# Turning the mix result over by four DMA transfers per unit instead of three GpSimd copies, one turn before its split

## The chip, the cores and the metric

The kernel runs on one NeuronCore of a Trainium2 chip. The metric is the device time of one execution in microseconds (us); the value of a kernel is the median of its runs. Five engines work side by side, each through its own list of instructions in order: TensorE (PE, with its weight loads as PEld), VectorE (DVE), ScalarE (ACT), GpSimd (POOL) and SyncE (SP). SP computes nothing here: it issues DMA transfers, one after the other, and an issue that has to wait for something holds up every issue behind it.

## The reference

A Fourier layer (real FFT over the sequence, a complex 256 x 256 mix with a soft threshold, inverse FFT) is followed by a token-shift channel mix and a second feed-forward with a mish activation:

```python
X = np.fft.rfft(x, axis=1)                       # x: 4 x 3072 x 256
Yr = Xr @ w_r - Xi @ w_i + b_r
Yi = Xr @ w_i + Xi @ w_r + b_i
Yr = np.sign(Yr) * np.maximum(np.abs(Yr) - lam, 0.0)   # Yi likewise
y = np.fft.irfft(Y, n=3072, axis=1)
...
k = np.maximum(xk @ w_k, 0.0); v = k * k @ w_v; r = sigmoid(xr @ w_r); x = r * v
...
h = x @ w_in; out = (h * np.tanh(softplus(h))) @ w_out
```

## The kernel before

The time falls into three stages: the first 302 us compute the Fourier layer up to the first half of the inverse transform, the rest computes the channel mix and then the last feed-forward. The change touches the first stage alone. A forward FFT of 3072 = 96 x 32 points is done in two steps of matrix products (`s1` over 96 rows, `s2` over 32), the inverse likewise (`is1`, then `is2`). Between `s1` and `s2`, and between `is1` and `is2`, the data goes through DRAM (`scr1`, `scr2`), which turns its layout. Every product of the first stage except `s1` is done in a split form: ACT rounds a tile to a high part (`Xh`, `Ah`, `Yh`), DVE computes the rest (`Xl`, `Al`, `Yl`), and PE multiplies high by high, high by low and low by high.

The work between the two DRAM passes is cut into 48 units (`NU`), 12 for each of 4 batches, and the loop at L687 runs one turn per unit, with several units in flight. In turn u, in the order of the program:

- `s2(u + 1)` (PE); `is1_ev(u - 3)` copies the inverse product of an earlier unit out of PSUM to `Cs` (ACT) and stores it to `scr2` (SP, L449); `s1_ev` evicts and stores a tile of a later batch;
- `s2_ev(u + 1)` splits the result of `s2` into `Xh` (ACT) and `Xl` (DVE); two steps of background work (`bg`, below);
- `load_A(u + 5)` (SP, L333) and `split_A(u + 3)`;
- `mix(u)`: the products with the mix weights and the bias (PE), `K1` (ACT) and the sum `yt` (DVE, L406);
- `split_Y(u - 1)`: `Yh` (ACT, L77) and `Yl` (DVE, L78); `above(u)`: `yc` (ACT, L411); `shrink(u)`: the soft threshold `Y` (DVE, L417) and its rearrangement;
- in 20 of the turns `s1` of a tile of a later batch with `load_x` (SP, L276); `is1(u - 2)` (PE, L436); two more steps of `bg`; from turn 33 on one step of `early`, which already loads and prepares the first tiles of the second stage.

The rearrangement is what the change is about. After `shrink`, `Y` holds in 128 partitions x 2 x 256 four quarters of 64 partitions x 256, and `is1` needs the upper quarter of column block 0 and the lower quarter of column block 1 exchanged. Three GpSimd copies through a helper tile `sw` do it in place (L419 to L421).

Two tables set the order around this. `bg` takes the weights of the second stage from a queue, one at a time: a DMA of 512 KB into `dec_raw` (SP, L111) in one step, then four steps later, one turn of the loop, the first of seven DVE instructions that decode it (L118 to L137), then the split (L97, L99). There are nine such weights in this stage, so nine DMAs, each issued in the last step of a turn (turns 4, 8, ... 36) and first read on DVE in the last step of the next turn, right behind `shrink`. `early(0)` in turn 33 loads `Dp`, `D` and `ift` (L457, L471, L252), `early(1)` splits two of them in turn 34.

PSUM holds one buffer for `s2` and one for `is1`, so PE starts `s2` of the next unit only when `Xl` of the last one has been read out, and `is1` only when `Cs` has been copied.

Of the kernel before, what the change touches and what calls it, by code (L numbers as in the profile page):

```python
# [8 lines left out]
F32 = mybir.dt.float32  # L9
# [4 lines left out]
ALU = mybir.AluOpType  # L14
# [3 lines left out]
B, S, D, FK, FF = 4, 3072, 256, 1024, 2048  # L18
N1, N2 = 96, 32
NG = 12  # L20
NU = B * NG
# [4 lines left out]
LAM = 0.01  # L26
# [3 lines left out]
def kernel(  # L30
# [27 lines left out]
    nc = tc.nc  # L58
# [13 lines left out]
    def split(src, hi, lo, lo_eng=None, hi_eng=None):  # L72

        if hi_eng is nc.vector:
            nc.vector.tensor_copy(out=hi, in_=src)
        else:
            nc.scalar.copy(out=hi, in_=src)  # L77
        (lo_eng or nc.vector).tensor_tensor(out=lo, in0=src, in1=hi, op=ALU.subtract)  # L78
# [6 lines left out]
    def bg(n):  # L85

        while n > 0 and bgq:
            try:
                next(bgq[0])
                n -= 1  # L90
            except StopIteration:
                bgq.popleft()
# [63 lines left out]
    p1p = p1.__enter__()  # L156
# [20 lines left out]

    def load_consts():
        def t(tag):
            return p1p.tile([128, 512], F32, tag=tag, name=tag, bufs=1)  # L180

        if not cst:
            cst["m"] = t("dec_raw")
            nc.sync.dma_start(out=cst["m"], in_=c_mw)
            return
        cst["x"] = [t("yt"), t("yc")]
        for v, w in zip(cst["x"], (w_r, w_i)):
            nc.sync.dma_start(out=v.rearrange("p (h n) -> p h n", h=2), in_=w.rearrange("(h p) n -> p h n", p=128))
# [17 lines left out]

    def split_mix():
        r, i = cst["x"]
        d = [p1p.tile([128, 512], F32, tag="T", name="wd", bufs=2) for _ in range(2)]
        nc.vector.scalar_tensor_tensor(out=d[1], in0=r, scalar=-1.0, in1=i, op0=ALU.mult, op1=ALU.subtract)  # L210
        nc.vector.tensor_tensor(out=d[0], in0=i, in1=r, op=ALU.subtract)
        for c, v in ((0, r), (2, d[1]), (1, d[0])):
            v = v.rearrange("p (h n) -> p h n", h=2)
            split(v, WX[:, :, c, 0, :], WX[:, :, c, 1, :])
# [64 lines left out]
    def load_x(b, q):  # L279
        new_x(b, q)  # L280
        for _ in x_loads(b, q):
            pass

    def warm(n):
        z = p1p.tile([128, 512], F32, tag="yt", name="zero", bufs=1)
        nc.vector.memset(z[:, 0:256], 0.0)
        p = ps1p.tile([128, 2, 512], F32, tag="s2", name="warm", bufs=1)
        for _ in range(n):
            nc.tensor.matmul(out=p[:, 0, 0:256], lhsT=z[:, 0:128], rhs=z[:, 0:256], start=True, stop=True)
# [34 lines left out]
    def gview(scr, g):  # L324

        return scr.rearrange("s n d -> (s n) d")[256 * g:256 * (g + 1)].rearrange("(e p) d -> p e d", e=2)
# [3 lines left out]
    def load_A(u):  # L330
        b, g = divmod(u, NG)
        t = p1p.tile([128, 2, D], F32, tag="A", name="A", bufs=4)
        nc.sync.dma_start(out=t, in_=gview(scr1a if u < 4 else scr1[b], g))  # L333
        A_t[u] = t
# [7 lines left out]
    def s2(u):  # L342
        last = u % NG == GS
        hl = Ah.pop(u)
        p = ps1p.tile([128, 2, 512], F32, tag="s2", name="s2p", bufs=1)
        for dh in range(2):
            v = p[:, dh, 0:384].rearrange("p (c e j) -> p c e j", c=3, e=2)
            for e in range(2):
                mc = MC[:, int(last and e == 1)]
                for i, (a, w) in enumerate(((0, 0), (0, 1), (1, 0))):  # L350
                    nc.tensor.matmul(  # L351
                        out=v[:, :, e, :], lhsT=hl[a][:, e, dh * 128:(dh + 1) * 128],
                        rhs=mc[:, w, :], start=(i == 0), stop=(i == 2),
                    )
        s2_t[u] = p
# [22 lines left out]
    mx_t, Y_t = {}, {}  # L378

    def mix(u):  # L380
        hl = Xh.pop(u)
        last = u % NG == GS
        p = ps1p.tile([128, 2, D], F32, tag="mx", name="mxp")
        k1 = ps1p.tile([128, D], F32, tag="k1", name="k1p", bufs=1)

        def terms(c, w):
            return [
                (hl[a][:, dh, 128 * c:128 * c + 128], WX[:, dh, w, b, :])
                for dh in range(2) for (a, b) in ((0, 0), (0, 1), (1, 0))
            ]  # L390

        def put(out, ts, start, stop=True):
            for i, (a, w) in enumerate(ts):
                nc.tensor.matmul(out=out, lhsT=a, rhs=w, start=(start and i == 0), stop=(stop and i == len(ts) - 1))  # L394

        put(k1, terms(2, 0), True)
        nc.tensor.matmul(out=p, lhsT=SEL[:, int(last), :], rhs=BR, start=True, stop=False)
        put(p[:, 0, :], terms(1, 2), False, False)
        ts = terms(0, 1)
        if last:  # L400
            ts += [(ZV[:, a, dh, :], WX[:, dh, 0, b, :]) for dh in range(2) for (a, b) in ((0, 0), (0, 1), (1, 0))]
        put(p[:, 1, :], ts, False)
        ks = p1p.tile([128, D], F32, tag="K1", name="K1", bufs=1)
        nc.scalar.copy(out=ks, in_=k1)
        t = p1p.tile([128, 2, D], F32, tag="yt", name="yt", bufs=1)
        nc.vector.tensor_tensor(out=t, in0=p, in1=ks.unsqueeze(1).to_broadcast([128, 2, D]), op=ALU.add)  # L406
        mx_t[u] = t

# [4 lines left out]

    def shrink(u):
        t, up = mx_t.pop(u)
        y = Y_t[u] = p1p.tile([128, 2, D], F32, tag="T", name="Y", bufs=2)
        nc.vector.scalar_tensor_tensor(out=y, in0=t, scalar=LAM, in1=up, op0=ALU.add, op1=ALU.min)  # L417
        w = p1p.tile([64, D], F32, tag="sw", name="sw", bufs=1)
        nc.gpsimd.tensor_copy(out=w, in_=y[64:128, 0, :])  # L419
        nc.gpsimd.tensor_copy(out=y[64:128, 0, :], in_=y[0:64, 1, :])  # L420
        nc.gpsimd.tensor_copy(out=y[0:64, 1, :], in_=w)  # L421

    def split_Y(u):
        yh = p1p.tile([128, 2, D], F32R, tag="Yh", name="Yh", bufs=2)
        yl = p1p.tile([128, 2, D], F32R, tag="Yl", name="Yl", bufs=2)
        split(Y_t.pop(u), yh, yl)
        Yh[u] = (yh, yl)

    def is1(u):
        b, g = divmod(u, NG)  # L430
        yh, yl = Yh.pop(u)
        p = ps1p.tile([128, 2, D], F32, tag="i1", name="i1p", bufs=1)
        parts = ((0, slice(0, 2)),) if g != GS else ((0, slice(0, 1)), (1, slice(1, 2)))
        for k, es in parts:
            for i, (w, v) in enumerate(((0, yh), (0, yl), (1, yh))):
                nc.tensor.matmul(  # L436
                    out=p[:, es, :], lhsT=WC[:, k, w, :], rhs=v[:, es, :], start=(i == 0), stop=(i == 2)
                )
        i1_t[u] = p
# [3 lines left out]
    def is1_ev(u):  # L443
        b, g = divmod(u, NG)
        p = i1_t.pop(u)
        tag, n = ("Cs", 2) if u < NU - 3 else ("A", 4)
        st = p1p.tile([128, 2, D], F32, tag=tag, name="Cs", bufs=n)
        nc.scalar.copy(out=st, in_=p)
        nc.sync.dma_start(out=gview(scr2[b], g), in_=st)  # L449
# [234 lines left out]

    later = {}
    U_E = 32
    for u in range(NU + 3):  # L687
        if 0 < u < NU - 1:
            s2(u + 1)
        if u > 2:  # L690
            is1_ev(u - 3)
        if s1_t:
            s1_ev()

        def fill():
            while s1_t:
                s1_ev()
            if u > 2:
                bg(2)

        if 0 < u < NU - 1:
            s2_ev(u + 1, fill)
        else:
            fill()
        if u + 5 < NU:
            load_A(u + 5)
        if 0 < u < NU - 3:
            split_A(u + 3)
        if u < NU:
            mix(u)  # L710
        if NU <= u < NU + 2:
            early(u - U_E - 2)
        if 1 <= u <= NU:
            split_Y(u - 1)
        if u < NU:
            above(u)
            shrink(u)
        if u == 0:
            load_x(1, 6)
        if u in S1_AT:  # L720
            i = 8 + S1_AT[u]
            s1(*divmod(i, 8))
            if i + 3 < 8 * B:
                load_x(*divmod(i + 3, 8))
        if 2 <= u < NU + 2:
            is1(u - 2)
        if u > 2:
            bg(2)
        if u == U_E:
            p1s.__exit__(None, None, None)  # L730
            pEg = tc.tile_pool(name="pE", bufs=1, side="left", reuse_waits="tile")
            pE[0] = pEg.__enter__()
        if U_E < u < NU - 1:
            early(u - U_E - 1)
# [425 lines left out]
    for P in range(2, 8 * NBLK + LAG):  # L1160
        t, q = divmod(P, 8)
# [111 lines left out]
```

## Time and profile before

| | |
|---|---|
| median of 3 runs | 1983.23 us (1983.07 to 1985.38) |
| profiled execution | 1983.62 us, of which the span of the profile is 1981.8 us |
| PE, PEld busy | 1962.0 us (99%), 1861.4 us (94%) |
| DVE, ACT, POOL busy | 1486.5 us (75%), 1154.0 us (58%), 106.7 us (5%) |
| granted TensorE clock, mean | 0.997 of full speed |
| DMA | 123.03 MB, mean 62 GB/s; 0.9 of the 16 engines' time in the first slice, 0.6 in the next three, 0.5 and less later |
| chain that ended last | PE 95%, DVE 2%, DMA 1%, ACT 1% |

PE is busy nearly always, over the whole span. What a change in the first stage is worth can therefore be read only where PE stands still in it, and from what it waits for there. The profile's line numbers are those of the kernel before; behind the change the lines from L420 on are one lower.

### The profile page before, as it was taken

Reading aid. Unit: us, or ns where it says so; the run is one execution under the profiler, and the core shown is the slowest. Engines: PE = TensorE matmul, PEld = TensorE weight load, DVE = VectorE, ACT = ScalarE, POOL = GpSimd, SP = SyncE. Lnnn points to the kernel's source line nnn. Section 1 sums busy time; section 2 is a strip of 40 time slices with the busy share of each in tenths; the row PEclk is TensorE's granted clock in tenths of the full one; section 3 lists DMA queues with packets and bytes.
Section 4 is the critical chain, followed back from the end, with each engine's and each line's share of the span. In section 5 each row is a group of like instructions: output and inputs, shape, how many; then the busy total and the mean of one; then the engine's idle time right before and its main releaser. Section 6 shows DMA issues by size and latency. Waiting matters only on the chain.

```text
span 1981.8 us, 33049 instructions
## 1 busy us (share of the span) xinstructions
PE 1962.0 (99%) x12946; PEld 1861.4 (94%) x12946; DVE 1486.5 (75%) x2413; ACT 1154.0 (58%) x1765; POOL 106.7 (5%) x196
## 2 busy tenths in 40 slices
PE   7999999999999999999999999999999999999999
PEld 5999989999999999999899999999999999999998
DVE  4788896776767767775587787777787777887785
ACT  3777777777777777776544444444444444544444
POOL 1222230000000000000000000000000000000000
PEclk9999999999999999999999999999999999999999
DMA  9666532221212212110110010010010010000000
GB/s 293 205 206 202 171 100 68 64 66 51 67 62 61 67 51 69 60 52 33 38 33 22 24 31 22 22 33 23 25 30 22 22 33 22 27 28 22 22 12 22
DMA packets 71744, 123.03 MB, mean 62 GB/s; under 512 B 6370, under 2 KB 48580, under 8 KB 71588
## 3 DMA queue, kind: packets, MB, share of 16 engines
q1 hardware_dynamic: 68004, 108.33, 18.3%
q0 software_dynamic: 3584, 12.58, 1.6%
q8 instruction: 102, 1.67, 0.4%
q14 instruction: 54, 0.44, 0.1%
HBM read 70.56 MB, written 50.33 MB: 61 GB/s over the span
## 4 chain that ended last, share of the span: by engine, by line
PE 95%; DVE 2%; DMA 1%; ACT 1%; issue 0%; POOL 0%; SPq 0%; DVEq 0%; ACTq 0%; POOLq 0%
PE h L1089 20%; PE o L1137 18%; PE kp L835 14%; PE vp L873 13%; PE o L1138 9%; PE pp L812 3%; PE p L1089 3%; PE mxp L394 3%; PE pp L518 3%; PE s2p L351 2%; PE s1p L296 2%; PE k1p L394 1%; PE i1p L436 1%; PE hp L778 1%; DMA XS<-in_x_dram 1%
## 5 line engine op out<-in xcount | busy, mean ns | idle before, releaser
L1137 PE MATMUL o<-WO,gh 128*128 128x512 f32 x1536 | 562.0, 394 | 0.0
L1138 PE MATMUL o<-WO,gl 128*128 128x256 f32 x1536 | 430.3, 280 | 0.0
L1089 PE MATMUL h<-xS,WS 128*128 128x256 f32 x2208 | 350.9, 281 | 0.0
L1102 ACT COPY p1s<-p 128x256 f32<-128x256 f32 x184 | 68.9, 375 | 471.3 <-PE p L1089 470.4
L1137 PEld LDWEIGHTS o<-WO,gh 128*128 128x128 f32 x1536 | 288.9, 188 | 43.3
L1089 PEld LDWEIGHTS h<-xS,WS 128*128 128x128 f32 x2208 | 299.6, 188 | 16.1
L835 PE MATMUL kp<-xk,WK 128*128 128x384 f32 x1536 | 290.9, 337 | 0.0
L1138 PEld LDWEIGHTS o<-WO,gl 128*128 128x128 f32 x1536 | 289.5, 188 | 0.2
L873 PE MATMUL vp<-kh,WV 128*128 128x384 f32 x1024 | 281.4, 336 | 0.0
L835 PEld LDWEIGHTS kp<-xk,WK 128*128 128x128 f32 x1536 | 267.6, 189 | 0.3
L1092 DVE TENSOR_TENSOR C<-h,p1s 128x512 f32<-128x512 f32 x184 | 127.2, 691 | 157.6 <-PE h L1089 157.6
L860 DVE TENSOR_TENSOR kl<-kr,kh 128x768 fp32r<-128x768 f32 x128 | 122.8, 959 | 160.1 <-ACT kr L859 158.2
L1074 DVE TENSOR_TENSOR gl<-g,gh 128x1024 fp32r<-128x1024 f32 x184 | 223.8, 1216 | 2.1 <-ACT g L1071 2.1
L1070 ACT ACTIVATE gh<-C 128x1024 fp32r<-128x1024 f32 x184 | 195.7, 1064 | 10.8 <-DVE C L1092 10.7
L1071 ACT ACTIVATE g<-C 128x1024 f32<-128x1024 f32 x184 | 193.1, 1049 | 0.0
L1089 PE MATMUL h<-xS,WI 128*128 128x256 f32 x1104 | 189.8, 280 | 0.0
L1092 DVE TENSOR_TENSOR C<-h,wu 128x512 f32<-128x512 f32 x368 | 187.8, 553 | 0.3 <-PE h L1089 0.3
L873 PEld LDWEIGHTS vp<-kh,WV 128*128 128x128 f32 x1024 | 186.3, 188 | 0.2
L873 PE MATMUL vp<-kl,WV 128*128 128x384 f32 x512 | 171.5, 335 | 0.0
L858 ACT ACTIVATE kh<-kr 128x768 fp32r<-128x768 f32 x128 | 108.4, 847 | 89.0 <-PE vp L873 88.8
L1089 PEld LDWEIGHTS h<-xS,WI 128*128 128x128 f32 x1104 | 155.7, 188 | 0.0
L1092 DVE TENSOR_TENSOR wu<-h,C 128x512 f32<-128x512 f32 x184 | 126.7, 689 | 35.3 <-PE h L1089 31.4
(181 smaller groups left out, 3056.5 us busy)
## 6 DMA issues: line engine op xcount, KB each, us to landing
scr<-Cs SPq DMA_DIRECT2D x48, 256.0 KB
D<-scr SPq DMA_DIRECT2D x32, 384.0 KB
x2d<-r POOLq DMA_DIRECT2D x32, 384.0 KB, 3.7
x<-x2d SPq DMA_DIRECT2D x24, 512.0 KB
out_dram<-ob SPq DMA_DIRECT2D x96, 128.0 KB
A<-scr SPq DMA_DIRECT2D x44, 256.0 KB
xs<-in_x_dram SPq DMA_DIRECT2D x24, 384.0 KB
scr<-xs SPq DMA_DIRECT2D x24, 384.0 KB
```

Of the source, the lines that this page charges most:

```text
L394: nc.tensor.matmul(out=out, lhsT=a, rhs=w, start=(start and i == 0), stop=(stop and i == len(ts) - 1))
L835: nc.tensor.matmul(out=p[:, m, 0:TA], lhsT=WK[:, dh, w, f * 128:(f + 1) * 128], rhs=hl[:, v, dh, :], start=(i == 0), stop=(i == 5),)
L858: nc.scalar.activation(out=kh, in_=kr, func=AF.Square)
L860: nc.vector.tensor_tensor(out=kl, in0=kr, in1=kh, op=ALU.subtract)
L873: nc.tensor.matmul(out=p[:, o, 0:TA], lhsT=WV[:, f, w, o * 128:(o + 1) * 128], rhs=v[:, m, :], start=(f == 0 and i == 0), stop=(f == 7 and ...
L1070: nc.scalar.activation(out=gh, in_=c, func=AF.Mish)
L1071: nc.scalar.activation(out=g, in_=c, func=AF.Mish)
L1074: nc.vector.tensor_tensor(out=gl, in0=g, in1=gh, op=ALU.subtract)
L1089: nc.tensor.matmul(out=out, lhsT=a(l), rhs=xS[:, v, b, :], start=(n == 0), stop=(n == 2))
L1092: nc.vector.tensor_tensor(out=out, in0=x0, in1=x1, op=ALU.add)
L1137: nc.tensor.matmul(out=o[m], lhsT=gh[:, m2, ms], rhs=WO[:, f], start=(f == 0), stop=False)
L1138: nc.tensor.matmul(out=o[m][:, 0, :], lhsT=gl[:, m2, ms], rhs=WO[:, f, 0, :], start=False, stop=(f == 15))
```

## The change

The threshold is now written in place into `yt` (two buffers instead of one), and four transfers of 64 partitions x 256 (64 KB each), issued by SP, carry the four quarters from `yt` to their places in a separate `Y` tile (three buffers instead of two). `sw` and the GpSimd copies are gone. `split_Y`, `is1` and `is1_ev` come one turn later, so the loop has one turn more.

```diff
     def load_consts():
         def t(tag):
-            return p1p.tile([128, 512], F32, tag=tag, name=tag, bufs=1)
+            return p1p.tile([128, 512], F32, tag=tag, name=tag, bufs=2 if tag == "yt" else 1)
...
-        d = [p1p.tile([128, 512], F32, tag="T", name="wd", bufs=2) for _ in range(2)]
+        d = [p1p.tile([128, 512], F32, tag="T", name="wd", bufs=3) for _ in range(2)]
...
-        z = p1p.tile([128, 512], F32, tag="yt", name="zero", bufs=1)
+        z = p1p.tile([128, 512], F32, tag="yt", name="zero", bufs=2)
...
-        t = p1p.tile([128, 2, D], F32, tag="yt", name="yt", bufs=1)
+        t = p1p.tile([128, 2, D], F32, tag="yt", name="yt", bufs=2)
...
     def shrink(u):
         t, up = mx_t.pop(u)
-        y = Y_t[u] = p1p.tile([128, 2, D], F32, tag="T", name="Y", bufs=2)
-        nc.vector.scalar_tensor_tensor(out=y, in0=t, scalar=LAM, in1=up, op0=ALU.add, op1=ALU.min)
-        w = p1p.tile([64, D], F32, tag="sw", name="sw", bufs=1)
-        nc.gpsimd.tensor_copy(out=w, in_=y[64:128, 0, :])
-        nc.gpsimd.tensor_copy(out=y[64:128, 0, :], in_=y[0:64, 1, :])
-        nc.gpsimd.tensor_copy(out=y[0:64, 1, :], in_=w)
+        nc.vector.scalar_tensor_tensor(out=t, in0=t, scalar=LAM, in1=up, op0=ALU.add, op1=ALU.min)
+        y = Y_t[u] = p1p.tile([128, 2, D], F32, tag="T", name="Y", bufs=3)
+        for e in range(2):
+            for c in range(2):
+                nc.sync.dma_start(out=y[64 * c:64 * c + 64, e, :], in_=t[64 * e:64 * e + 64, c, :])
...
-    for u in range(NU + 3):
+    for u in range(NU + 4):
         if 0 < u < NU - 1:
             s2(u + 1)
-        if u > 2:
-            is1_ev(u - 3)
+        if u > 3:
+            is1_ev(u - 4)
...
-        if 1 <= u <= NU:
-            split_Y(u - 1)
+        if 2 <= u < NU + 2:
+            split_Y(u - 2)
...
-        if 2 <= u < NU + 2:
-            is1(u - 2)
+        if 3 <= u < NU + 3:
+            is1(u - 3)
```

The first place where the order of instructions moves is SP's list in turns 32 and 33, where the eighth of the nine weights is loaded (`dec_raw`), followed by the first loads for the second stage (`Dp`, `D`, `ift`). A turn begins with the store of `Cs`. Before:

```order
L449 DMA scr_2_64<-Cs 128x2x256
L333 DMA A<-scr_3_60 128x2x256
L111 DMA dec_raw<-in_moe_w_v_dram 128x2x512
L449 DMA scr_2_64<-Cs 128x2x256
L333 DMA A<-scr_3_60 128x2x256
L457 DMA Dp<-scr_0_62 96x256
L471 DMA D<-scr_0_62 96x1024
L252 DMA ift<-in_c_if_dram 96x384
```

and in the changed kernel:

```order
L448 DMA scr_2_64<-Cs 128x2x256
L333 DMA A<-scr_3_60 128x2x256
L420 DMA Y<-yt 64x256 x4
L111 DMA dec_raw<-in_moe_w_v_dram 128x2x512
L448 DMA scr_2_64<-Cs 128x2x256
L333 DMA A<-scr_3_60 128x2x256
L420 DMA Y<-yt 64x256 x4
L456 DMA Dp<-scr_0_62 96x256
L470 DMA D<-scr_0_62 96x1024
L252 DMA ift<-in_c_if_dram 96x384
```

The load of the weight and the three loads of `early(0)` stood behind nothing but the loads of their turn; now each stands behind the four transfers of `Y`, and these cannot be issued before DVE has finished `shrink` of the same turn. The same holds for `load_x` and for all nine `dec_raw` loads.

The second place is the end of the loop on ACT, where the last units leave (`Yh` is the last split, `Cs` the copy out of PSUM behind `is1`, `yT` and `ya` are `early`). Before:

```order
L77 CAST Yh<-Y 128x512
L411 ACTIVATE yc<-yt 128x512
L448 COPY Cs<-i1p 128x512
L528 COPY yT<-yT 128x3x32 x2
L531 COPY ya<-s1p 128x192
L528 COPY yT<-yT 128x3x32 x2
L531 COPY ya<-s1p 128x192
L77 CAST Yh<-Y 128x512
L448 COPY Cs<-i1p 128x512
L531 COPY ya<-s1p 128x192 x2
L448 COPY Cs<-i1p 128x512
```

and in the changed kernel:

```order
L77 CAST Yh<-Y 128x512
L411 ACTIVATE yc<-yt 128x512
L447 COPY Cs<-i1p 128x512
L527 COPY yT<-yT 128x3x32 x2
L530 COPY ya<-s1p 128x192
L527 COPY yT<-yT 128x3x32 x2
L530 COPY ya<-s1p 128x192
L77 CAST Yh<-Y 128x512
L447 COPY Cs<-i1p 128x512
L530 COPY ya<-s1p 128x192 x2
L77 CAST Yh<-Y 128x512
L447 COPY Cs<-i1p 128x512 x2
```

One more `Yh` stands at the end: behind the last `early` copies there is now the last split with two copies of `Cs`, and the last `is1` on PE needs the first of these two.

## Rows read from the trace of the kernel before

**Rows 1.** Busy time of each engine in stretches of the span (us, from its start).

```profile
core 0: us, PE busy (x) PEld busy (x) DVE busy (x) ACT busy (x) POOL busy (x), PEclk, DMA share, GB/s
...
40.00:302.00 262.00, 255.34 (x1834) 236.45 (x1834) 217.89 (x348) 186.72 (x373) 75.00 (x145) 0.99 0.59 180
302.00:1981.80 1679.80, 1675.57 (x10982) 1603.31 (x10981) 1253.10 (x2039) 953.06 (x1367) 24.57 (x33) 1.00 0.13 38
...
60.00:220.00 160.00, 160.00 (x1147) 148.25 (x1146) 128.41 (x197) 115.66 (x229) 41.08 (x86) 1.00 0.67 203
220.00:300.00 80.00, 75.13 (x549) 69.52 (x549) 73.73 (x125) 56.42 (x117) 28.06 (x49) 0.98 0.41 127
235.90:239.50 3.60, 3.58 (x17) 3.58 (x18) 3.47 (x6) 1.33 (x2) 0.00 (x0) 0.53 0.00 1
```

**Rows 2.** What PE waited for: us in total, times, longest us.

```profile
PE s2p L351 <- DVE Xl L78: 5.7, 6, 1.9
```

**Rows 3.** PE's timeline at 235.9 us: start, duration, engine, line, idle before and its end.

```profile
235.92 0.58 PE L351 MATMUL s2p<-MC,Ah 128*128 128x192 f32 x2 [1.82 <-DVE Xl L78]
```

**Rows 4.** DVE's timeline: thresholds and first decode instructions of three weights.

```profile
222.28 0.69 DVE L417 SCALAR_TENSOR_TENSOR Y<-yt,yc 128x512 f32<-128x512 f32 x1
...
225.98 0.69 DVE L78 TENSOR_TENSOR Yl<-Y,Yh 128x512 fp32r<-128x512 f32 x1 [0.34 <-ACT Yh L77]
...
227.19 0.42 DVE L118 TENSOR_SCALAR dec_v<-dec_raw 128x512 int32<-128x512 int32 x1
...
243.98 0.69 DVE L417 SCALAR_TENSOR_TENSOR Y<-yt,yc 128x512 f32<-128x512 f32 x1
...
249.13 0.43 DVE L118 TENSOR_SCALAR dec_v<-dec_raw 128x512 int32<-128x512 int32 x1
...
310.26 0.43 DVE L118 TENSOR_SCALAR dec_v<-dec_raw 128x512 int32<-128x512 int32 x1 [0.95 <-DMA dec_raw<-in_moe_w_in_dram]
```

**Rows 5.** SP's timeline: issues of transfers, with the time that an issue took.

```profile
214.62 0.32 SPq L312 DMA_DIRECT2D scr<-xs  x1
217.67 0.36 SPq L333 DMA_DIRECT2D A<-scr  x1
...
219.50 0.46 SPq L111 DMA_DIRECT2D dec_raw<-in_moe_w_v_dram  x1
...
303.93 0.42 SPq L111 DMA_DIRECT2D dec_raw<-in_moe_w_in_dram  x1
```

**Rows 6.** What ACT and DVE waited for: us in total, times, longest us.

```profile
ACT Yh L77 <- POOL Y L421: 12.7, 16, 1.5
...
DVE Xl L78 <- ACT Xh L77: 25.9, 26, 2.4
...
DVE Yl L78 <- ACT Yh L77: 2.0, 4, 0.8
...
DVE dec_v L118 <- DMA dec_raw<-in_moe_w_k_dram: 0.4, 1, 0.4
```

**Rows 7.** The end of the loop: timelines of PE, then DVE, then ACT.

```profile
295.86 0.40 PE L436 MATMUL i1p<-Yh,WC 128*128 128x512 f32 x1
...
296.56 0.25 PE L518 MATMUL s1p<-ifh,Dh 96*128 96x192 f32 x1
...
302.63 5.17 PE L835 MATMUL kp<-xk,WK 128*128 128x384 f32 x24
...
297.86 0.68 DVE L417 SCALAR_TENSOR_TENSOR Y<-yt,yc 128x512 f32<-128x512 f32 x1
...
300.03 0.62 ACT L77 CAST Yh<-Y 128x512 fp32r<-128x512 f32 x1 [0.68 <-POOL Y L421]
```

**Rows 8.** Timelines of DVE and POOL at 224.36 us; then `Al` by its tile: ns min/median/max.

```profile
224.36 0.68 DVE L78 TENSOR_TENSOR Al<-A,Ah 128x512 fp32r<-128x512 f32 x1
...
224.36 0.94 POOL L421 COPY Y<-sw 64x256 f32<-64x256 f32 x1
...
L78 DVE TENSOR_TENSOR Al<-A,Ah x48: 674/687/911, 30.4 to 284.2; 128x512 fp32r<-128x512 f32 x48
```

## The prediction

> **What bounds the kernel now.** I began with the busy times by stretch, because PE's 99% over the whole span says nothing of one stage. They show where there is anything to win or to lose: behind 302 us PE is idle for 4.2 us of 1679.8, and the change does not touch that part; in the loop, from 40 to 302 us, it is idle for 6.7 us of 262 [rows 1]. Within the loop there are two regimes. From 60 to 220 us PE has no idle time that the view shows (160.00 of 160), while DVE is busy for 128.4, ACT for 115.7 and POOL for 41.1 us. From 220 to 300 us PE is idle for 4.9 us of 80, and DVE is busy for 73.7 [rows 1]. The list of waits then says for whom PE stands still: for `Xl` on DVE, 5.7 us in six waits [rows 2], the longest at 234.1 to 235.9 us [rows 3]. In the stretch right behind that wait the granted clock is 0.53, about the lower of its two levels (1.2 of 2.4 GHz) [rows 1]; 3.6 us at that clock lose some 1.7 us of matmul time. On DVE's timeline the instructions around that wait stand back to back but for a few tenths (I read 222 to 250 us; the largest gap is the 0.34 us before 225.98) [rows 4]. So the order of DVE's list sets the time between 220 and 295 us, and PE sets it before. Whatever makes DVE later in the second regime is paid in full; in the first, DVE has (160 - 128.4), about 32 us in some 29 turns, or 1.1 us per turn, to give away.
>
> **The change part by part.** The sum is made against the profiled execution, 1983.62 us, which lies 0.39 above the median of the runs.
>
> *Removed: 144 GpSimd copies.* They are nearly all of POOL's 75.0 us in the loop [rows 1], and lie beside other work. On a path they lie only where somebody waits for them: ACT does so for 12.7 us, in 16 turns [rows 6]. But ACT is not the bound, and DVE waited for the `Yh` behind them for 2.0 us in all [rows 6], of which 0.34 us fall into the stretch that DVE bounds [rows 4]; the rest lies where PE has work or in the tail, below. I take -0.3, bounds -2.0 and 0.
>
> *Moved: the extra turn.* DVE, ACT and PE execute the same instructions as before. One `is1` moves from the middle of the loop behind its end: three matmuls, 295.86 to 296.56, 0.7 us of PE [rows 7]. That changes nothing in the sum of PE's work: 0, and in the tail the whole loop arrives 0.7 us earlier. With an extra turn (4.4 to 6 us) a unit's transfers have time to land before `Yh`, so I charge nothing for their own latency, except in the tail, where no other units cover it.
>
> *Added: 192 transfers of 64 KB.* An issue costs SP about 0.45 us (rows show 0.32 to 0.46) [rows 5], four of them 1.8 us per turn of at least 4.4. SP computes nothing, so the price lies in what stands behind them. They wait for `shrink`, and behind them, in program order, stand `load_x`, the nine weight loads and the loads of `early(0)`. Before, SP could run ahead: the eighth weight was issued at 219.50, 2.8 us before the threshold of its turn even began (222.28), and DVE read it at 227.19, right behind the next threshold, 7.7 us after the issue [rows 4, 5]. Now it can be issued only at 222.28 + 0.69 + 1.8 = 224.8. What does such a load take from issue to landing? Below there is the 384 KB store at 214.62, for which the `A` load at 217.67 waited: 3.05 us. Above there is the 512 KB load issued at 303.93, which DVE awaited until 310.26: 6.3 us, behind one 256 KB store, in the quiet traffic of the next stage [rows 4, 5]. The second is nearer in size and kind, but includes a late straggler that need not recur, so I take the middle, 4.7 us: landing at 229.5 instead of being there at 227.19, **+2.3 us** of DVE (bounds +0.7 and +3.9). The ninth weight repeats it: threshold at 243.98 + 0.69 + 1.8 = 246.5 for the issue, landing 251.2 against 249.13, **+2.1 us** (bounds +0.4 and +3.7). Both fall into DVE's regime, and behind the waiting decode stands the next `Xl`, for which PE waits. Both count in full: +4.4.
>
> The Trainium skill (DMA: Bandwidth & Descriptors, Anatomy of one DMA) gives a transfer about 2.0 us plus its bytes at 436 GB/s. By that estimate the 512 KB load would take 3.2 us, the two stalls would be 0.8 and 0.6, and the sum 1.7 instead of 4.7; the measured 6.3 us speaks against it, and it is kept as a rival.
>
> The other seven weights (turns 4 to 28) come as late. There DVE has its 1.1 us per turn, and it waits for `Xh` before `Xl` anyway (25.9 us in 26 waits, up to 2.4) [rows 6]; PE needs that `Xl` only a turn later. I charge 0; without that cover each stall of 2.2 us would cost PE 1.1. `load_x` comes three tiles, over four turns, ahead of use: 0. `Dp` and `ift` come some 5 us later, but ACT, which reads them in the next turn, is shifted by the first stall too: 0, at worst +0.5.
>
> *The tail.* The last threshold ends at 297.86 + 0.68 = 298.54; before, `Yh` began at 300.03 [rows 7]. Now the last of four issues stands at about 299.9. For its landing the nearest bounds are 1.0 us (below: no more than an issue and first bytes, an estimate from the 0.45) and the store's 3.05 us; I take 2.1, so 302.0. Then `Yh` 0.6 us, and, because ACT's order has the next-to-last `Cs` behind it, that copy another 0.5, before PE may begin the last `is1`: 303.2, and `kp` at 303.9 instead of 302.63 [rows 7]. Less the 0.7 us by which all arrives earlier: **+0.6**, bounds 0 and +1.6.
>
> *The clock.* Longer waits of PE may bring the lower clock once more, 1.7 us. In DVE's regime a slower PE fills time in which it would wait; I take 0, upper bound +1.7.
>
> Sum: -0.3 + 4.4 + 0.6 = **+4.7 us**, so 1988.3 for such an execution, **1987.9 us** as a median. The bounds add up to (-2.0 + 1.1 + 0) = -0.9 and (7.6 + 0.5 + 1.6 + 1.7) = +11.4, but hardly all at one end.
>
> **The rivals.**
> *The loads land in time (0.31).* If a weight load takes the store's 3.05 us, the stalls are 0.7 and 0.4, and with -0.3 and a tail of +0.3 the sum is +1.1: 1984.3, no change to be told. For it: the store's row [rows 5]. Against it: one weight of the first regime was awaited for 0.4 us although it had been issued early [rows 6], and so was the one at 310.26.
>
> *GpSimd was what made DVE late (0.07), faster.* Then everything PE loses between 220 and 300 us is to be had: 4.9 us idle and the 1.7 us of the clock, 6.6 in all, 1976.6. It decides if DVE's own durations or starts hang on the copies. Where an `Al` and the third copy start together, at 224.36, DVE takes its usual 0.68 us and the copy 0.94; of 48 `Al` the median is 687 ns and the longest 911 [rows 8]. And DVE is busy for 73.7 of 80 us [rows 1] with its own work; that leaves little. The Trainium skill (SBUF — State Buffer, Who interferes with whom) speaks for this rival: a DVE instruction with two SBUF inputs contends with a GpSimd instruction that reads SBUF, and the loser is held up entirely. By that rule up to POOL's 28.1 us in this stretch [rows 1] could hold DVE up; the pair at 224.36 says that GpSimd was the loser.
>
> *The transfers choke the queue (0.10), much slower.* The DMA engines are busy for 0.67 of 60 to 220 us [rows 1], and each turn gets another 256 KB. If `load_x`, `Y` and the weights come so late that the seven early stalls are not covered, each costs PE the 1.1 us above: 7.7 more, 1995.6. Against it: most loads there have a turn or more to spare.
>
> **How the numbers follow.** Forecast 0.52, the rivals 0.31, 0.07 and 0.10. A measurement of this kernel tells about 0.2%, 4 us, from no change: the lines are 1979.3 and 1987.2. The forecast lies just above the upper one; of its 0.52 I put 0.40 above and 0.12 below it. Slower: 0.40 + 0.10 = 0.50; same: 0.31 + 0.12 = 0.43; faster: 0.07. The range leaves out the faster rival and most of the choked queue and takes the rest with its bounds: from 1982.3 (the sum's -0.9) to 1993.0 (the stalls' upper bounds, 7.6, with the tail's 1.6, half of the clock's 1.7 and the -0.3).
>
> **What would show it.** In the changed profile POOL is all but idle in the loop, and ACT waits for no copy. DVE should show two waits for `dec_raw` of some 2 us at its L118, near 227 and 249 us, each followed by a longer wait of PE for `Xl`; the SP view should show both loads issued behind four `Y` transfers, at 224 to 225 and 246 to 247. `kp` should begin 4 to 5 us later than 302.63. The prediction is wrong if those decode instructions start without a wait (then the loads land sooner than I think), if PE's idle time grows before 220 us (choked queue), or if DVE's instructions get shorter without the copies.

## The result and the profile after

The changed kernel takes 2008.05 us (median of 4 runs, 2007.29 to 2009.68) against 1983.15 us before: ratio 1.0120, interval 1.0108 to 1.0132, 24.9 us slower. Slower was forecast, but by 4.7 us, and the time lies 15 us above the range. Times here and below are medians of all runs; one of the eight executions of the version with the transfers on GpSimd's queue took 4588.25 us, and its ratio is taken without it.

The profiled execution has a span of 2006.6 us, 24.8 more than before. The first two fences cut the loop into the same three pieces of work in both kernels: from unit 0's first bias matmul to unit 33's, from there to unit 47's, and from there to the first matmul of the next stage (`kp`). Before:

```profile
core 0: us, PE busy (x) PEld busy (x) DVE busy (x) ACT busy (x) POOL busy (x), PEclk, DMA share, GB/s
41.30:222.70 181.40, 181.39 (x1303) 168.38 (x1304) 144.73 (x222) 129.58 (x256) 45.89 (x96) 1.00 0.68 204
222.70:294.20 71.50, 67.51 (x496) 62.74 (x495) 67.35 (x111) 50.60 (x102) 25.46 (x42) 0.98 0.41 126
294.20:302.60 8.40, 7.01 (x40) 5.77 (x39) 5.74 (x19) 5.24 (x16) 2.39 (x6) 0.90 0.25 85
```

and after (behind the three pieces: the first piece up to the end of its longest wait, the stretch behind that wait, the stretch behind the wait at 246.46, and all that follows the loop):

```profile
42.10:239.50 197.40, 186.99 (x1298) 169.48 (x1299) 143.50 (x221) 126.54 (x255) 0.00 (x0) 0.98 0.79 224
239.50:316.10 76.60, 69.42 (x499) 64.25 (x498) 66.11 (x111) 49.91 (x102) 0.00 (x0) 0.96 0.62 172
316.10:326.80 10.70, 8.02 (x44) 6.25 (x43) 6.89 (x20) 6.33 (x18) 0.00 (x0) 0.87 0.59 169
42.10:177.50 135.40, 125.61 (x885) 113.56 (x885) 95.03 (x146) 86.04 (x174) 0.00 (x0) 1.00 0.80 226
177.50:184.30 6.80, 6.78 (x31) 6.69 (x32) 6.60 (x12) 3.12 (x6) 0.00 (x0) 0.52 0.88 265
249.20:256.00 6.80, 6.71 (x31) 6.61 (x32) 5.91 (x12) 2.82 (x6) 0.00 (x0) 0.52 0.76 213
...
327.00:2006.60 1679.60, 1675.66 (x10981) 1603.71 (x10979) 1251.63 (x2036) 951.98 (x1367) 24.50 (x33) 1.00 0.13 38
```

The three pieces grew by 16.0, 5.1 and 2.3 us; the rest is 0.8 ahead of unit 0 and 0.6 behind the loop. The loss has two forms. PE's idle time (length less busy) went from 0.01 to 10.41, from 3.99 to 7.18 and from 1.39 to 2.68 us, together 14.9 more. PE's busy time went up by 5.6, 1.9 and 1.0 us, together 8.5. Some 4.8 of these are the granted clock, an estimate from the rows: twice it is 0.52, about the lower of the two levels, for 6.8 us from where PE resumes after a long wait, which loses 3.3 and 3.2 us, against 1.7 for the one such stretch before [rows 1]; in the last piece the lower level costs about the same in both. The rest shows in turns with a wait at the full clock, about a quarter of a us in each (73.68 to 80.36 us after: 5.42 busy and 1.26 idle; the same turn before, 73.55 to 78.70: 5.15 busy); why was not found. Most of the loss lies in the piece in which PE had not been idle at all.

The list of waits after says for whom the engines stood still (us in total, times, longest us):

```profile
PE s2p L351 <- DVE Xl L78: 18.8, 16, 4.1
DVE dec_v L118 <- DMA dec_raw<-in_moe_w_k_dram: 15.0, 4, 4.3
DVE dec_v L118 <- DMA dec_raw<-in_moe_w_v_dram: 14.1, 4, 5.4
DVE dec_v L118 <- DMA dec_raw<-in_moe_w_r_dram: 2.2, 1, 2.2
...
ACT Yh L77 <- DMA Y<-yt: 1.7, 2, 1.3
ACT ifh L77 <- DMA ift<-in_c_if_dram: 1.6, 1, 1.6
```

The first row answers to [rows 2]: 5.7 has become 18.8 us. The three `dec_raw` rows answer to the last of [rows 6]: one wait of 0.4 us has become nine, one for every weight, of 15.0 + 14.1 + 2.2 = 31.3 us. ACT's 12.7 us of waits for the GpSimd copies are gone. The chain that ended last now leads through SP's issues and their transfers, where it was PE 95%, DVE 2%, DMA 1%, ACT 1% before:

```profile
PE 88%; DMA 4%; DVE 3%; SPq 2%; ACT 1%; issue 1%; POOL 0%; DVEq 0%; ACTq 0%
```

How one such wait arises is seen on SP's timeline, 240 to 243 us, and on DVE's, 239 to 249 us:

```profile
240.36 2.44 SPq L420 DMA_DIRECT2D Y<-yt  x4
242.84 0.59 SPq L111 DMA_DIRECT2D dec_raw<-in_moe_w_v_dram  x1
```

```profile
239.34 0.69 DVE L416 SCALAR_TENSOR_TENSOR yt<-yt,yc 128x512 f32<-128x512 f32 x1
...
243.40 0.69 DVE L416 SCALAR_TENSOR_TENSOR yt<-yt,yc 128x512 f32<-128x512 f32 x1
247.94 0.43 DVE L118 TENSOR_SCALAR dec_v<-dec_raw 128x512 int32<-128x512 int32 x1 [3.85 <-DMA dec_raw<-in_moe_w_v_dram]
```

The threshold of unit 32 ends at 240.03, four issues take 2.44 us, the weight is issued at 242.84 and has landed at 247.94, 5.1 us later. DVE was ready for it at 244.09, behind the next threshold, and stood for 3.85 us; behind that stands the `Xl` for which PE waits, on PE's timeline 2.83 us:

```profile
249.29 0.74 PE L351 MATMUL s2p<-MC,Ah 128*128 128x192 f32 x2 [2.83 <-DVE Xl L78]
```

The longest of the nine waits, 5.41 us at 176.17, has a longer history. SP's timeline before it, SP's own waits from 156 to 164 us, and PE's row behind it:

```profile
157.76 0.42 SPq L312 DMA_DIRECT2D scr<-xs  x1
162.39 0.36 SPq L333 DMA_DIRECT2D A<-scr  x1
162.85 2.39 SPq L420 DMA_DIRECT2D Y<-yt  x4
165.33 0.53 SPq L448 DMA_DIRECT2D scr<-Cs  x1
165.91 1.81 SPq L333 DMA_DIRECT2D A<-scr  x1
167.76 2.40 SPq L420 DMA_DIRECT2D Y<-yt  x4
170.26 0.53 SPq L276 DMA_DIRECT2D xs<-in_x_dram  x1
170.83 0.44 SPq L111 DMA_DIRECT2D dec_raw<-in_moe_w_v_dram  x1
```

```profile
SPq L333 <- DMA scr<-xs: 4.1, 1, 4.1
```

```profile
177.52 0.74 PE L351 MATMUL s2p<-MC,Ah 128*128 128x192 f32 x2 [4.14 <-DVE Xl L78]
```

The `A` load at 162.39 had to wait 4.1 us for a store, and everything behind it waited along. From there SP goes from one issue to the next with hardly a gap, two turns' transfers among them, and does not catch up before the weight. DVE then stood for 5.41 us and PE for 4.14. Nearly half of the 16.0 us is lost here: the two turns from 170.85 to 188.79 take 17.94 us, in the kernel before 10.57 (162.99 to 173.56).

### The profile page after: what moved, and what is told of

Read it like the earlier page. It is cut to its first block, busy times and chain, and to the rows that moved or that the text cites. A ratio compares the mean times of both kernels' runs of the same rounds, so it can differ in the third digit from the quotient of the medians.

```text
span 2006.6 us, 33154 instructions
## 1 busy us (share of the span) xinstructions
PE 1974.8 (98%) x12946; PEld 1868.4 (93%) x12946; DVE 1483.8 (74%) x2413; ACT 1149.5 (57%) x1765; POOL 32.8 (2%) x52
## 4 chain that ended last, share of the span: by engine, by line
PE 88%; DMA 4%; DVE 3%; SPq 2%; ACT 1%; issue 1%; POOL 0%; DVEq 0%; ACTq 0%
PE h L1088 20%; PE o L1136 18%; PE kp L834 14%; PE vp L872 13%; PE o L1137 9%; PE pp L811 3%; PE p L1088 3%; PE pp L517 3%; DMA Y<-yt 3%; SPq L420 2%; PE mxp L394 1%; PE s2p L351 1%; DVE yt L406 1%; PE s1p L296 1%; DMA XS<-in_x_dram 1%; PE hp L777 1%
## 5 line engine op out<-in xcount | busy, mean ns | idle before, releaser
L1069 ACT ACTIVATE gh<-C 128x1024 fp32r<-128x1024 f32 x184 | 195.7, 1064 | 10.7 <-DVE C L1091 10.6
```

What stands on the lines that cost most here:

```text
L1069: nc.scalar.activation(out=gh, in_=c, func=AF.Mish)
```

## The experiments

Theory **Q**: what costs is the place in SP's list. The weight loads (and the loads of `early(0)`) stand behind the threshold and four issues, DVE and ACT wait for them, and PE for those two. Theory **T**: it is the traffic; 12.6 MB more through the DMA engines make all loads land late. Theory **L**: it is the extra turn and the deeper buffers. Ratios are against the kernel before, run on the same chip (1983.9 to 1984.2 us), with 95% intervals.

### The extra turn alone

The kernel before with the new buffers and loop order, but with its GpSimd copies:

```diff
-    for u in range(NU + 3):
+    for u in range(NU + 4):
...
-        if 1 <= u <= NU:
-            split_Y(u - 1)
+        if 2 <= u < NU + 2:
+            split_Y(u - 2)
```

> The changed loop (one turn more until the split, three and two buffers), but with the three GpSimd copies in place of the four transfers. It measures the extra turn alone. Theories Q and T: the turn costs or gains little, ACT's wait of 12.7 us for the copies goes, the time is that of before within 2 us (1982 to 1985). Theory L: most of the 25 us is here, 2000 or more.

Measured 1983.43 us, ratio 0.9996 (0.9986 to 1.0006). L falls. ACT no longer waits for the copies here either, and nothing is gained by it that can be told from noise.

### The four transfers behind the weight load

The transfers leave `shrink` and are issued at the end of the turn's background work, behind `load_x` and the weight:

```diff
         if u > 2:
             bg(2)
+        if u < NU:
+            turn_Y(u)
```

> The changed kernel, with the four transfers of a unit issued at the end of its turn, behind load_x and the weight load instead of ahead of them; nothing else moves. Theory Q (the place in SP's list: the weight load stands behind shrink and four issues of 0.64 us, and DVE awaits it, 31.3 us in nine waits): the weight loads are issued early again, the nine waits of DVE for dec_raw shrink from 31.3 us to under 6, and the time falls from 2008.0 to 1983 to 1989. Theory T (traffic and issue time of 192 more transfers, wherever they stand): the loads still land late, at least half of the 25 us stays, 1997 or more. Theory L (the extra turn, its tail and the lower clock): unchanged within 4 us of 2008.

Measured 1992.45 us, ratio 1.0045 (1.0030 to 1.0060): the loss falls from 24.9 to 8.4 us with every byte still moving. DVE's waits for weights fall from 31.3 to 12.8 us. Both are short of what Q expected. The loads of `early(0)` still stand behind the transfers, and there PE's longest wait now lies (4.1 us, for ACT's `Cs`).

### The four transfers on GpSimd's queue

```diff
-                nc.sync.dma_start(out=y[64 * c:64 * c + 64, e, :], in_=t[64 * e:64 * e + 64, c, :])
+                nc.gpsimd.dma_start(out=y[64 * c:64 * c + 64, e, :], in_=t[64 * e:64 * e + 64, c, :])
```

> The changed kernel, with the four transfers issued by GpSimd, which has nothing else to do in this stage, instead of SP. SP's list is then that of the kernel before. Theory Q: the waits of DVE for dec_raw go to about 1 us as before, 1982 to 1988. Theory T: the same 256 KB a turn run on the same 16 engines, so the waits stay at 15 us or more and the time at 1997 or above. A third way: if GpSimd's issues are slow, Yh waits for Y, and ACT shows it.

Measured 1989.83 us, ratio 1.0025 (1.0014 to 1.0036). Weight waits are down to 4.3 us, with the same bytes. Instead `Y` itself comes late: ACT waits 24.3 us for it, in 19 turns. T is hard to hold from here on.

### The weights decoded a turn later

Order and transfers as in the changed kernel; only the decode stands eight background steps, two turns, behind its load (likewise for the `w_k` and `w_v` weights):

```diff
-    bgq.append(bg_weight(p1p, src, WR[:, :, 0, :], WR[:, :, 1, :], 2))
+    bgq.append(bg_weight(p1p, src, WR[:, :, 0, :], WR[:, :, 1, :], 2, 8))
```

> The changed kernel as it is, SP's order and all transfers included, but each of the nine weights of the first stage is decoded two turns behind its load instead of one (eight steps of background work between instead of four). It takes away DVE's wait alone. Theory Q: the waits for dec_raw fall from 31.3 us to under 3 and the time to 1984 to 1992. If the transfers hurt in other ways as well (late A tiles, late Y, SP blocked behind a store), that part stays; theory T expects 1997 or more.

Measured 1997.11 us, ratio 1.0071 (1.0056 to 1.0086). That is above Q's range, and by the number alone it would do for T; where the time is lost decides. The first piece of the loop, by its windows:

```profile
42.60:225.30 182.70, 181.57 (x1298) 167.51 (x1299) 137.70 (x209) 127.66 (x253) 0.00 (x0) 1.00 0.81 238
```

182.7 us against 197.4, and 181.4 before: DVE's waits for the weights are the whole of the 16.0 us but for 1.3, the lower clock included. DVE is busy for less because part of the decoding has moved into the later pieces. There this version takes 91.0 us against 79.9: with that work added to DVE, and a wait of PE (3.5 us) where ACT waits for `Dp` and `ift`.

### The same, with the loads of early(0) ahead of the transfers

```diff
+        if u == U_E + 1:
+            load_Dp(0)
+            load_D(0)
+            load_IF(0)
         if u < NU:
             mix(u)
```

> The kernel with the weights decoded two turns behind their load, and in addition the three loads of early(0) (Dp, D, ift) issued a turn's work earlier, ahead of the transfers of Y of their turn. Theory Q says that the rest of 13 us is the same thing at a second place: ACT awaited Dp and ift for 1.8 and 2.3 us and PE stood for 3.5 us behind it at 237 us. Then that wait goes and the time falls by 3 to 5 us, from 1997.1 to 1992 to 1994; what then remains against 1984 is the tail (2 us) and the decode work that this kernel moved to the end. If the rest is traffic, the time stays at 1997 within 1 us.

Measured 1995.95 us, ratio 1.0061 (1.0046 to 1.0076): 1.2 us better where I expected 3 to 5. ACT still waits 2.9 us for `ift`, and PE for ACT (2.5). In this version the late decodes crowd the same turns, so it can't tell what the early loads cost; the pair of runs further down can.

### One row of 1 KB behind the threshold

The kernel before, with one tiny transfer on SP that waits for `shrink` and that nobody reads:

```diff
+        nc.sync.dma_start(out=row[u:u + 1, :], in_=y[0:1, 0, :])
```

> The kernel before, with its GpSimd copies and without the extra turn, and one transfer of a single row (1 KB, to a scratch row in DRAM) issued by SP behind shrink, where the four transfers of Y stand in the changed kernel. It adds the wait of SP's list for shrink, 0.6 us of issue per turn and no traffic to speak of. Theory Q: the weight load is issued some 0.7 us behind shrink instead of 2.7, lands some 5.5 us behind it, and DVE waits for it in the shorter turns: 5 to 13 us of waits in all, 1985 to 1992. Theory T (traffic and issue time): no waits, 1984 within 1 us.

Measured 1984.80 us, ratio 1.0002 (0.9993 to 1.0011). The wait for the threshold alone makes DVE stand for weights (5.5 us in five waits, the longest 1.8), and it costs nothing that shows: stalls of this size are covered, as the prediction thought. The five awaited weights land 4.2 to 5.7 us behind their issue; the nine of the changed kernel take 4.1 to 5.7. So the bytes of `Y` do not make the weights land later; they are issued later.

### Nine rows of 1 KB behind the threshold

```diff
+        for j in range(9):
+            nc.sync.dma_start(out=row[9 * u + j:9 * u + j + 1, :], in_=y[j:j + 1, 0, :])
```

> The kernel before, GpSimd copies kept, no extra turn, and behind each threshold nine transfers of one row of 1 KB, which nothing reads: at 0.29 us per issue 2.6 us on SP's list, as the four large ones take, but 9 KB instead of 256 KB per unit. Theory Q, if the place in the list is all: the weights are issued as late as in the changed kernel, DVE waits for them for 20 to 31 us, and the time is 1998 to 2008. Theory T (the bytes make the weights land late): at most the 5.5 us of waits of the run with one row and 1984 to 1987.

Measured 2018.45 us, ratio 1.0173 (1.0157 to 1.0188), above what even Q expected. SP's timeline around one weight, DVE's row behind it, and the window of the first piece of work:

```profile
178.01 2.91 SPq L420 DMA_DIRECT2D row<-Y  x9
...
181.39 0.43 SPq L112 DMA_DIRECT2D dec_raw<-in_moe_w_v_dram  x1
...
183.42 6.09 SPq L420 DMA_DIRECT2D row<-Y  x9
```

```profile
186.68 0.43 DVE L119 TENSOR_SCALAR dec_v<-dec_raw 128x512 int32<-128x512 int32 x1 [6.92 <-DMA dec_raw<-in_moe_w_v_dram]
```

```profile
42.90:253.30 210.40, 192.26 (x1304) 173.85 (x1304) 144.57 (x222) 129.42 (x257) 45.11 (x96) 0.96 0.58 174
```

9 KB per unit instead of 256, GpSimd copies and loop as before, a DMA share of 0.58 (before 0.68), and the same picture: DVE waits 41.7 us for the nine weights, and the piece takes 210.4 us. T is not needed for this: the time is lost without the bytes, by issues alone. It is more than the changed kernel loses, because nine rows take 2.9 us and, where other issues are dense, up to 6.09.

### Eight transfers of 32 partitions

```diff
             for c in range(2):
-                nc.sync.dma_start(out=y[64 * c:64 * c + 64, e, :], in_=t[64 * e:64 * e + 64, c, :])
+                for h in (0, 32):
+                    nc.sync.dma_start(out=y[64 * c + h:64 * c + h + 32, e, :], in_=t[64 * e + h:64 * e + h + 32, c, :])
```

> The same 256 KB per unit in eight transfers of 32 partitions instead of four of 64. Theory Q (issues on SP's list stand ahead of the weight load): eight issues at a pitch of 0.45 to 0.64 us take 3.6 to 5.1 us instead of 2.5, so each of the nine weights is 1.1 to 2.6 us later than in the changed kernel; nothing covers that any more, so DVE's waits at L118 grow from 31 to some 41 to 54 us and the time from 2008 to between 2018 and 2035. Theory T (the bytes moved set it): the bytes are the same, 2008 within 2 us.

Measured 2097.03 us, ratio 1.0566 (1.0550 to 1.0582). The direction is Q's, the size far above its 2018 to 2035. The issues of this run by their line (ns min/median/max), then of the changed kernel:

```profile
L421 SPq DMA_DIRECT2D Y<-yt x384: 507/589/1917, 47.5 to 411.7; - x192
```

```profile
L420 SPq DMA_DIRECT2D Y<-yt x192: 461/594/2407, 46.7 to 322.1; - x192
```

Half a transfer takes as long to issue as a whole one. Eight of them fill some 4.8 us of a turn of 4 to 6 in which SP has up to five other issues, so SP has hardly time left in a turn. Besides the weights (78.1 us) ACT waits 49.5 us for `Y`:

```profile
ACT Yh L77 <- DMA Y<-yt: 49.5, 24, 4.1
DVE dec_v L118 <- DMA dec_raw<-in_moe_w_k_dram: 37.1, 4, 10.3
DVE dec_v L118 <- DMA dec_raw<-in_moe_w_v_dram: 33.4, 4, 10.4
```

### Two transfers and two GpSimd copies

Only the two quarters that change place go by DMA:

```diff
-            for c in range(2):
-                nc.sync.dma_start(out=y[64 * c:64 * c + 64, e, :], in_=t[64 * e:64 * e + 64, c, :])
+            c = 1 - e
+            nc.sync.dma_start(out=y[64 * c:64 * c + 64, e, :], in_=t[64 * e:64 * e + 64, c, :])
+            nc.gpsimd.tensor_copy(out=y[64 * e:64 * e + 64, e, :], in_=t[64 * e:64 * e + 64, e, :])
```

> The changed kernel with two transfers per unit instead of four: only the two quarters that change place are transferred, the two that stay are copied by GpSimd. The weight loads still stand behind shrink, but behind 1.3 us of issues instead of 2.6 and half the bytes. Theory Q with the issue time as its main part: the nine waits of DVE fall by about 1.3 us each, from 31.3 to some 20 us, and the time by 9 to 13 us to 1995 to 1999. If the wait for shrink alone were the cause, the time stays within 4 us of 2008.

Measured 1987.81 us, ratio 1.0017 (1.0008 to 1.0027). Half the issues leave half the stalls (15.2 us in nine waits, the longest 3.1), but not half the loss: 3.6 of 24.9 us, and the time is far below the 1995 to 1999 expected. The loss isn't proportional to the stalls. Up to about 3 us each, with some four turns from one to the next, they are nearly covered; the granted clock stays at 1.00 from unit 0 on (41.93 to 307.6 us).

### The weight loads on GpSimd's queue, without and with the loads of early(0) ahead

```diff
-            nc.sync.dma_start(out=fv(raw.rearrange("p n w -> p (n w)")), in_=src.bitcast(I32))
+            (nc.gpsimd if pool is p1p else nc.sync).dma_start(out=fv(raw.rearrange("p n w -> p (n w)")), in_=src.bitcast(I32))
```

Without:

> The changed kernel with the nine weight loads issued by GpSimd, and nothing else; the three loads of early(0) stay behind the four transfers. Against the run with both moved (1986.7) it tells what the late Dp and ift cost: by theory Q for these too ACT waits for ift for some 1.7 us and the time is 1988 to 1990; if ACT's wait is covered, 1986.7 within 1.

Measured 1992.21 us, ratio 1.0040 (1.0027 to 1.0052). The profiled execution took 2000.26 us; in it PE also stood for 4.78 us up to 55.60, while ACT waited for an `A` load, early in the first piece. PE's and ACT's rows around 248 us:

```profile
248.79 0.79 PE L435 MATMUL i1p<-Yh,WC 128*128 128x512 f32 x1 [5.52 <-ACT Cs L447]
```

```profile
244.46 0.40 ACT L77 CAST Dph<-Dp 96x256 fp32r<-96x256 f32 x1 [2.33 <-DMA Dp<-scr]
247.74 0.51 ACT L77 CAST ifh<-ift 96x384 fp32r<-96x384 f32 x1 [2.88 <-DMA ift<-in_c_if_dram]
```

With:

> The changed kernel with the four transfers on SP as they are, but the nine weight loads of the first stage issued by GpSimd, which is idle there, and the loads of early(0) ahead of the transfers of their turn. Nothing that an engine needs soon then stands behind shrink on SP but load_x. Theory Q: DVE's waits for dec_raw under 6 us, 1985 to 1989. Theory T: 1997 or more. All the 12.6 MB of Y still move.

Measured 1986.66 us, ratio 1.0016 (1.0007 to 1.0026). No wait for a weight is left in the loop, and all 12.6 MB still move. The two medians differ by 5.5 us, and their intervals leave some 2 to 8: that is what the late `Dp` and `ift` cost once DVE's stall no longer covers them. In the two profiled executions the second piece takes 77.3 and 70.6 us. In the changed kernel itself ACT waited 1.6 us there.

### Besides, the last two units turned over by GpSimd

```diff
+        if u >= NU - 2:
+            y = Y_t[u] = p1p.tile([128, 2, D], F32, tag="T", name="Y", bufs=3)
+            nc.vector.scalar_tensor_tensor(out=y, in0=t, scalar=LAM, in1=up, op0=ALU.add, op1=ALU.min)
+            w = p1p.tile([64, D], F32, tag="sw", name="sw", bufs=1)
+            nc.gpsimd.tensor_copy(out=w, in_=y[64:128, 0, :])
+            nc.gpsimd.tensor_copy(out=y[64:128, 0, :], in_=y[0:64, 1, :])
+            nc.gpsimd.tensor_copy(out=y[0:64, 1, :], in_=w)
+            return
```

> The run with the weight loads on GpSimd's queue and early(0) ahead (1986.7), and besides the last two of the 48 units rearranged by the three GpSimd copies of the kernel before. There PE stands still for 1.97 us at 303.64 before the last is1 but one, because ACT's Yh waits for the transfers of the last unit. If that wait is what the tail costs, it falls by 1.4 to 2.0 us and the time is 1984.7 to 1985.3, about that of the kernel before. Rival: something else (the last Cs, the clock) sets the end there, and it stays within 0.5 of 1986.7.

Measured 1983.38 us, ratio 1.0000 (0.9991 to 1.0009), below the 1984.7 to 1985.3 expected. The three pieces of work of this run:

```profile
42.70:224.50 181.80, 181.07 (x1297) 167.57 (x1298) 144.16 (x221) 128.88 (x256) 5.17 (x8) 1.00 0.84 248
224.50:295.00 70.50, 66.40 (x499) 61.54 (x498) 65.78 (x111) 49.73 (x102) 0.71 (x1) 1.00 0.64 176
295.00:303.40 8.40, 7.06 (x43) 5.65 (x42) 6.67 (x20) 6.23 (x18) 2.38 (x6) 1.00 0.39 129
```

181.8, 70.5 and 8.4 us, the lengths of before within 1 us, with 46 of the 48 units still turned over by SP's transfers and the DMA engines busier than before. Nothing clear of noise is left of the loss. Each version taken against the kernel before of its own comparison, it falls from 24.9 us to 8.0 without the late weights, to 2.4 without the late early loads, and to -0.5 without the tail: 16.9, 5.5 and 2.9 us in this order, each with an uncertainty of some 3. No version came out faster than the kernel before.

## Why the prediction was wrong, step by step

- **Copies removed, -0.3; extra turn, 0.** Nothing speaks against either: the extra turn alone measured 0.9996. The removal of the copies was not measured alone.
- **The eighth and ninth weight, +4.4.** Mechanism and place are as predicted: the loads stand behind four `Y` issues, DVE waits at L118, PE for the next `Xl`. The sizes were low. Four issues take 2.4 us, not 1.8 (0.594 us each against the 0.45 read off larger loads), and the weight of the fence above landed 5.1 us behind its issue, not 4.7; so that stall was 3.85 us instead of 2.3. The ninth was 2.2 (predicted 2.1). The whole second piece lost 5.1, near the +4.4: the stalls were longer, 6.1 in all, a part of them was covered, and the lower clock came on top, so that closeness is in part luck.
- **The other seven weights, "I charge 0".** This is the step that failed. They cost the first piece 16.0 us, shown by taking their waits away (182.7 instead of 197.4). The fallback, 1.1 us per stall if the cover were gone, was too low as well: seven times 1.1 is 7.7. The seven waits were 15.0 + 14.1 - 3.85 = 25.2 us in all, 3.6 each and not 2.2; of these PE paid 10.4 in idle time, so cover there was, for 14.8, or 2.1 each and more than the 1.1. What was mis-sized is the stall. With 1.8 us stalls the term is 0, with up to 3.1 nearly so; behind the four stalls of 4.2 to 5.4 PE stood for 1.1 to 4.1 us at the next `Xl`, and the rest of the 16.0 is its longer busy time.
- **Why the stall was mis-sized.** The cost was reckoned from one turn at the end, where SP has time between turns. In the turns of five of these seven weights a `load_x` stands between the four transfers and the weight. SP's timeline from 92 us shows such a turn of the first piece, and DVE's row the decode of its weight:

```profile
92.27 2.39 SPq L420 DMA_DIRECT2D Y<-yt  x4
94.75 0.53 SPq L276 DMA_DIRECT2D xs<-in_x_dram  x1
95.32 0.44 SPq L111 DMA_DIRECT2D dec_raw<-in_moe_w_k_dram  x1
```

```profile
100.78 0.43 DVE L118 TENSOR_SCALAR dec_v<-dec_raw 128x512 int32<-128x512 int32 x1 [4.28 <-DMA dec_raw<-in_moe_w_k_dram]
```

  The threshold ended at 91.85, so the weight was issued 3.5 us behind it, not 1.8, and it landed 5.5 us behind its issue, not 4.7; DVE was ready at 96.50. Over the seven weights the issue follows the threshold of its turn by 2.6 to 4.2 us, once by 6.6 (the weight at 170.83, behind the `A` load that waited for a store), and the landing follows the issue by 4.75 to 5.7. The kernel before already had long issues there: its `w_k` weights, issued from 63.7 to 130.5 us, took 0.45 to 1.31 us to issue. What stands ahead of each weight in its own turn should have been added up.
- **The clock, 0, at most +1.7.** It was some 4.8 us, by the estimate above, and PE's busy time grew by 8.5 in all. A term that follows PE's idle time can't be bounded by one stretch when the idle time itself may grow.
- **`Dp` and `ift`, 0, at worst +0.5.** In the changed kernel ACT waited 1.6 us. Once the weights were out of the way they cost some 5.5 us: the argument that ACT is shifted too was right, but cover by another loss is no cover in a sum.
- **The tail, +1.3 without the 0.7.** It grew by 2.3 (8.4 to 10.7 us). The time from the last issue to `Yh` was right: the four last issues start at 320.28 and take 2.38, so the last begins at about 322.1, and `Yh` follows at 324.19, 2.1 us later, as taken. But the issues were slower, so that `Yh` began 4.1 us behind the threshold and not 3.5, and the last `is1` was priced at 0.7 us, while it took 1.45 (325.35 to 326.80) at the lower clock, as it had before (301.18 to 302.63).

Timelines of SP, ACT and PE in the tail of the changed kernel:

```profile
320.28 2.38 SPq L420 DMA_DIRECT2D Y<-yt  x4
```

```profile
324.19 0.62 ACT L77 CAST Yh<-Y 128x512 fp32r<-128x512 f32 x1 [1.34 <-DMA Y<-yt]
```

```profile
325.35 0.80 PE L435 MATMUL i1p<-Yh,WC 128*128 128x512 f32 x1 [1.91 <-ACT Cs L447]
```

Of the rivals, "the loads land in time" fell with the nine landings of 4.1 to 5.7 us. The 3.2 us that the prediction worked out from the Trainium skill's rule (DMA: Bandwidth & Descriptors, Anatomy of one DMA) are too short for these loads. The page gives the rule for a DMA that GpSimd issues, which the prediction did not say; these are issued by SP. "GpSimd was what made DVE late" fell too: DVE's busy time is 1483.8 us without the copies and 1486.5 with them. "The transfers choke the queue" came nearest. Its condition, seven early stalls not covered, is what happened, and its sign, idle time of PE before 220 us, came; its reason, busy DMA engines, was wrong (nine rows of 1 KB do the same), and its price was half of the real one.

That an issue which waits holds up the rest of its queue is shown by the rows at 157.76 to 162.85. The Trainium skill (DMA: Bandwidth & Descriptors, Anatomy of one DMA) gives the reason: a wait for a semaphore happens on the issuing sequencer, before the transfer is dispatched, and the DMA engines themselves wait for none.

## What to carry to other kernels

A DMA that waits for a late result is a barrier in its queue: before adding one, list what stands behind it in that queue and who reads that, and put loads that wait for nothing ahead of it or on another queue. Add up the issues of the densest turn by their durations in the trace, as for any other engine; the bytes can be harmless where the number of issues isn't. Cover is a store that is used up: compare the whole stall with it, and charge what exceeds it to every repetition, with the lower clock where one follows the wait.

## What was not expected of the hardware

- An issue on SP does not go by bytes: 0.594 us (median) for 64 partitions of 1 KB, 0.589 for 32 partitions, and 0.25 us (median) for a single row of 1 KB. The 512 KB weights of this stage take 0.43 to 0.59 in the changed kernel.
- The same issue can take far longer: up to 2.4 us for one `Y` transfer, and 6.09 instead of 2.91 us for nine rows. Both fall into turns with many issues; what holds SP there was not tried.
- After a wait of PE of 2.8 us (246.46 to 249.29) the granted clock stayed at 0.52 for 6.8 us; before, after 1.8 us, at 0.53 for 3.6 us [rows 1, 3]. Four waits of 1.1 to 1.65 us in the first piece (at 77.0, 82.9, 101.0 and 125.4 us) were not followed by it: the granted clock is 1.00 from 42.10 to 177.50. The two long stretches at the lower clock added some 4.8 us, net of the one before, to 14.9 us of idle time.
